# Attention and feed-forward on one core: the value products of a pair's fourth block and half block in one burst

## The chip, the core and the metric

One core of one Trainium2 chip runs the whole program. The metric is device time in microseconds (us), from the start of the program to its end. The engines are TensorE (PE: matrix products and transposes), VectorE (DVE), ScalarE (ACT), GpSimd (POOL) and SyncE (SP, which issues most of the transfers); each works through its own queue in order and waits for the others by semaphores.

## What is computed

Four batches of eight heads go through attention (queries are averaged two by two, so 576 rows of queries meet 1152 keys, with a head width of 64), and the result, 576 x 512 a batch, through a mixing step (the real part of a two-dimensional Fourier transform, added to its input), a normalisation and a feed-forward network of width 2048:

```python
def _attn_ref(q, k, v):
    q_pool = q.reshape(B, H, S // factor, factor, D).mean(axis=3)
    scores = scale * np.matmul(q_pool, k.transpose(0, 1, 3, 2))
    scores = scores - np.max(scores, axis=-1, keepdims=True)
    attn = np.exp(scores)
    attn = attn / (np.sum(attn, axis=-1, keepdims=True) + 1e-09)
    return np.matmul(attn, v)

def _moe_ref(x, w_ch1, w_ch2):
    mixed = np.real(np.fft.fft(np.fft.fft(x, axis=1), axis=2))
    u = x + mixed
    un = (u - np.mean(u)) / np.sqrt(np.var(u) + 1e-06)     # per row
    return u + np.maximum(un @ w_ch1, 0.0) @ w_ch2
```

All of it is float32; the weights come as 64 bit numbers and are converted on the chip.

## The kernel before

**Pairs and blocks.** The 32 heads are worked in 16 pairs (0 to 15). The 576 queries of a head are four blocks of 128 and a half block of 64. For block j = 0 to 3 each of the two heads has a tile of its own; for j = 4 the two half blocks share one tile. A tile goes through these steps:

- scores: three pieces of 384 keys, two products each (four for the half block's tile), L220, into slots of the PSUM pool `ps_t` (five slots); DVE copies each piece to the tile `sp` and takes the row's extreme (L222);
- exp of the whole 1152 columns on ACT (L234, `s_exp`), when all three pieces are there;
- transposes of 128 x 128 on PE (L247, `t_step`), four to a PSUM slot, each group copied to a tile `pt` (L250) by ACT, for the second head's second group by DVE. A block of two tiles has the groups 4, 4, 4, 4 and 2, the half block 4, 4 and 1. `pt` has six buffers;
- value products (L263, `av`): nine chunks of keys for each of the two heads, the first head into partitions 0 to 63 of the accumulator `po`, the second into 64 to 127. The moving side is 128 columns wide for a block and 64 for the half block. The only buffer of `ps_o` holds `po`; ACT copies it to `x` (L271).

The page calls the PSUM tiles by pool: `s` or `t` (pool `ps_t`), `f` (pool `ps_f`), `o` (the accumulator). PE's transposes of the first four pairs mostly go to `f`, later ones to `t`.

**The order.** It is written out by the generator `attention()`, one block after another: two score pieces of the next block, then `finish` (the value products of the block before), then the transposes of this block in groups, with two further score pieces of the next block after the first and after the second group, and at the end the exps of the next block (`exps()`). So the exp of a block stands on ACT behind the copies of the transposes of the block before, and on PE the transposes of a block have two score pieces of the next block and the value products of the block before ahead of them. In block 3 the next one is the half block, in the half block it is block 0 of the next pair.

**The planner.** Between the yields of `attention()` runs a planner. It keeps a clock `now` (nanoseconds, from the numbers that the generator yields, as 1950 for a block's value products and 1000 for the half block's), runs events whose time has come, as the softmax denominators' path (`den_recip`: a transpose D on PE at L280, two small transfers, and the multiplication of `x` by them), starts conversions of the weights (`convert`, from a clock of 60000 on, 32 in all, with ACT, DVE and POOL), and places work of finished batches: `mids` (Fourier step L505 and L513, normalisation L545 to L604) and `fills` (FFN blocks of 12 products, L699 to L701), the latter as far as `credit` goes, which grows with the yielded PE time. What is left of it stands behind the last pair.

**The conversions' buffers.** A conversion takes three tiles of 128 x 512 with the tag `cv` (four buffers) from the pool `cvp`. `todo` holds conversions that have not begun, `busy` those that run. In the trace, conversions run from pair 2 to pair 9.

Of the kernel before, what the change touches and what calls it, by code (L numbers as in the profile page):

```python
# [12 lines left out]
F32 = mybir.dt.float32  # L13
# [7 lines left out]
B, H, S, D = 4, 8, 1152, 64  # L21
# [3 lines left out]
P = 128  # L25
NKC = S // P
# [28 lines left out]
def fused_kernel(ctx: ExitStack, tc: tile.TileContext, k2, q2, v2, w1, w2, cst, out):  # L55
    nc = tc.nc
# [8 lines left out]
    ptp = pool("pt", 6)  # L65
    smp = pool("sm", 2)
    cvp = pool("cv", 1)
# [7 lines left out]
    ps_t = pool("ps_t", 5, space=PSUM)  # L75
    ps_o = pool("ps_o", 1, space=PSUM)
# [27 lines left out]
    qkv = {}  # L104
# [134 lines left out]
    def t_step(pr, items, eng):  # L239

        steps[0] += 1
        if pr < 4 and steps[0] % 5 != 2:
            ps = ps_f.tile([P, 512], F32, tag="f", name="f")
        else:
            ps = ps_t.tile([P, 512], F32, tag="t", name="t")
        for i, (k, c) in enumerate(items):
            nc.tensor.transpose(ps[:, i * P:i * P + P], sp[k][:, c * P:(c + 1) * P], ident)  # L247
        pt = ptp.tile([P, 512], F32, tag="pt", name="pt")
        o = len(items) * P
        (nc.vector.tensor_copy if eng == "v" else nc.scalar.copy)(pt[:, :o], ps[:, :o])  # L250
        return pt

    xt = {}
    started = []

    def av(pr, j, where):
        nonlocal now
        po = ps_o.tile([P, P], F32, tag="o", name="o")
        w = P if j < 4 else D
        for c in range(NKC):  # L260
            for y in range(2):
                pt, o = where[y, c]
                nc.tensor.matmul(po[y * D:y * D + D, :w], lhsT=qkv[2 * pr + y][3][:, c, :], rhs=pt[:, o:o + w],  # L263
                                 start=c == 0, stop=c == NKC - 1)
            if c in (2, 5) and j < 4:
                now += 650 * (c // 2)
                run_events()
                now -= 650 * (c // 2)
        if pr not in xt:
            xt[pr] = xt[pr + 1] = xp.tile([P, 2, SQ], F32, tag="x", name="x")  # L270
        nc.scalar.copy(xt[pr][:, pr % 2, j * P:j * P + w], po[:, :w])  # L271
# [40 lines left out]
    def attention():  # L312
# [35 lines left out]
        for i, (pr, j) in enumerate(units):  # L348
# [32 lines left out]
            def tr(items, eng):  # L381
                pt = t_step(pr, [(k, c) for k, c, _ in items], eng)
                for x, (_, _, ys) in enumerate(items):
                    for y, o in ys:
                        where[y, items[x][1]] = pt, x * P + o
                return 105 * len(items)
# [10 lines left out]
            if i:  # L397
                yield some(2)
                yield finish(*held)
# [12 lines left out]
            for k in tiles:  # L412
                sp.pop(k)
        yield finish(*held)

    def finish(pr, j, where):
        if j == 0 and pr % 2 == 0 and pr // 2 >= XB:

            drain(*divmod(pr // 2 - XB, 2))
        if j == 2 and pr % 2 and (pr + 1) // 2 >= XB and pr + 1 < NP:  # L420
            drain(*divmod((pr + 1) // 2 - XB, 2))
        av(pr, j, where)
        if j == 4:
            for y in range(2):
                qkv.pop(2 * pr + y)
        return 1950 if j < 4 else 1000


    ut = {}
# [234 lines left out]
    ORDER = [(w, q * GF + i) for q in range(NFC // GF) for w in range(2) for i in range(GF)]  # L664

    todo = deque(ORDER)
    busy = []
# [124 lines left out]
    now = due = credit = 0.0  # L792
# [11 lines left out]
    def run_events():  # L804
        while events and events[0][0] <= now:
            heapq.heappop(events)[2]()

    def drain(b, h):
        nonlocal now, due, credit
        while (b, 2 * h + 1) not in done_f2:  # L810
            if mids and now >= due:
                c = step(mids)
                if c:
                    now += c[0]
                    credit -= c[0]
                    due = now + c[1]
                continue
            c = step(fills)
            now += c or 300
            credit -= c  # L820
            conversions()
            run_events()
# [116 lines left out]
```

## Time and profile before

| | us |
|---|---|
| median of three runs | 1013.74 |
| the three runs | 1014.59, 1013.74, 1013.72 |
| the profiled execution | 1013.12 |
| its span, first to last instruction | 1011.4 |

| engine | busy us | share of the span |
|---|---|---|
| PE | 962.3 | 95% |
| DVE | 601.4 | 59% |
| ACT | 526.3 | 52% |
| POOL | 398.2 | 39% |

The pairs take the span up to 791 us, the rest of the feed-forward network the remaining 220. All times below are from the profiled execution and counted from its first instruction; what lies around the span (1.7 us) is no engine's work.

### The profile page before, as it was taken

The numbers are of one execution on the slowest core, as the hardware profiler recorded it, in microseconds if no ns is written. First come the engines' busy times: TensorE is split into PE (matmuls) and PEld (weight loads), VectorE is DVE, ScalarE is ACT, GpSimd is POOL, SyncE is SP. The second block draws the span as 40 slices with busy tenths as digits, with TensorE's granted clock in tenths as the row PEclk, the third lists the DMA queues.
The fourth block names the chain that finished last, engine by engine and source line by source line (L and its number), as shares of the span: only waits on it lengthen the run. The fifth ranks groups of instructions, "written<-read, shape, count | busy, mean of one in ns | idle before, by whom it ended". The sixth has DMA issues, their size and how long they took to land.

```text
span 1011.4 us, 19728 instructions
## 1 busy us (share of the span) xinstructions
PE 962.3 (95%) x7392; PEld 838.3 (83%) x7392; DVE 601.4 (59%) x1526; ACT 526.3 (52%) x1033; POOL 398.2 (39%) x577
## 2 busy tenths in 40 slices
PE   6999989798999998998999999999999999999998
PEld 5898888677788887776988888787988888899998
DVE  5557869789875597866544465745644275422222
ACT  5778868658865665655744454535844221301100
POOL 3555875868776667774523222222400000000000
PEclk9999999999999999999999999999999999999999
DMA  5645467556477775585765464354442445734432
GB/s 178 181 128 182 148 203 250 162 172 187 132 227 270 260 239 178 171 302 159 232 193 178 123 198 100 91 172 142 131 124 83 152 147 151 244 131 125 125 125 63
DMA packets 62515, 170.91 MB, mean 169 GB/s; under 512 B 16770, under 2 KB 20242, under 8 KB 62420
## 3 DMA queue, kind: packets, MB, share of 16 engines
q1 hardware_dynamic: 55924, 151.18, 47.5%
q0 software_dynamic: 4320, 17.70, 5.5%
q8 instruction: 58, 0.95, 0.4%
q10 hardware_dynamic: 2176, 0.79, 0.3%
q14 instruction: 37, 0.30, 0.1%
HBM read 146.88 MB, written 22.75 MB: 168 GB/s over the span
## 4 chain that ended last, share of the span: by engine, by line
PE 53%; DVE 2%; ACT 1%; issue 1%; POOL 0%; DVEq 0%; ACTq 0%
PE f L699 7%; PE f L701 6%; PE f L700 6%; PE s L220 6%; PE o L263 6%; PE t L247 5%; PE t L699 5%; PE t L701 5%; PE t L700 5%; DVE sp L222 1%; PE f L513 1%; PE t L513 1%; PE f L505 0%; ACT pt L250 0%; ACT sp L234 0%
## 5 line engine op out<-in xcount | busy, mean ns | idle before, releaser
L222 DVE TENSOR_SCALAR_CACHE_REDUCE sp<-s,bia 128x384 f32<-128x384 f32 x288 | 177.4, 616 | 88.0 <-PE s L220 65.2
L220 PE MATMUL s<-ks,qh 128*128 128x384 f32 x480 | 185.3, 386 | 16.9 <-ACT qh L164 6.1
L234 ACT ACTIVATE sp<-sp,bia 128x1152 f32<-128x1152 f32 x144 | 180.1, 1255 | 6.1 <-DVE sp L222 5.9
L250 ACT COPY pt<-t 128x512 f32<-128x512 f32 (+2 forms) x243 | 125.0, 527 | 109.6 <-PE t L247 108.3
L220 PE MATMUL s<-ks,ql 128*128 128x384 f32 x480 | 164.8, 343 | 2.6 <-POOL ql L197 2.6
L263 PE MATMUL o<-pt,vs 128*64 128x128 f32 (+1 forms) x2880 | 163.6, 267 | 1.4 <-DVE pt L250 1.2
L263 PEld LDWEIGHTS o<-pt,vs 128*64 128x64 f32 x2880 | 145.1, 138 | 23.4 <-issue 20.4
L247 PE MATMUL t<-ident,sp 128*128 128x128 f32 x1045 | 151.5, 277 | 7.2 <-ACT pt L250 3.5
L247 PEld LDWEIGHTS t<-ident,sp 128*128 128x128 f32 x1045 | 121.6, 141 | 28.0 <-issue 6.3
L189 POOL TENSOR_TENSOR ks<-kr,ks 64x288 fp32r<-64x288 f32 x120 | 99.3, 859 | 52.2 <-DMA ks<-in_k 21.6
L220 PEld LDWEIGHTS s<-ks,qh 128*128 128x128 f32 x480 | 92.6, 193 | 26.5 <-ACT qh L164 6.6
L220 PEld LDWEIGHTS s<-ks,ql 128*128 128x128 f32 x480 | 93.1, 194 | 3.8 <-POOL ql L197 2.8
L718 ACT ACTIVATE g<-f 128x512 fp32r<-128x512 f32 (+1 forms) x49 | 28.3, 577 | 120.1 <-PE f L701 120.1
L719 DVE SCALAR_TENSOR_TENSOR g<-f,g 128x512 fp32r<-128x512 f32 (+1 forms) x49 | 32.5, 663 | 97.0 <-ACT g L718 97.0
L197 POOL TENSOR_TENSOR ql<-qr,qh 128x288 fp32r<-128x288 f32 (+2 forms) x75 | 55.9, 770 | 77.2 <-ACT qh L194 76.2
L222 DVE TENSOR_SCALAR_CACHE_REDUCE sp<-s 128x384 f32<-128x384 f32 x144 | 78.6, 546 | 11.4 <-PE s L220 10.5
L653 POOL TENSOR_TENSOR rest<-rest,wa 128x256 f32<-128x256 f32 x64 | 50.0, 799 | 70.9 <-DVE wa L646 51.9
L699 PE MATMUL f<-g,w 128*128 128x512 f32 (+1 forms) x192 | 75.9, 396 | 2.0 <-PE f L585 1.0
L699 PE MATMUL f<-unh,w 128*128 128x512 f32 (+1 forms) x196 | 76.7, 391 | 0.9 <-DVE g L719 0.9
L701 PE MATMUL f<-unl,w 128*128 128x512 f32 (+1 forms) x196 | 74.6, 380 | 0.0
L700 PE MATMUL f<-unh,w 128*128 128x512 f32 (+1 forms) x196 | 74.2, 379 | 0.0
L701 PE MATMUL f<-g,w 128*128 128x512 f32 (+1 forms) x192 | 74.0, 385 | 0.0
(146 smaller groups left out, 1723.4 us busy)
## 6 DMA issues: line engine op xcount, KB each, us to landing
w<-w SPq DMA_DIRECT2D x128, 512.0 KB, 4.2
qr<-in_q SPq DMA_DIRECT2D x30, 576.0 KB, 5.8
ks<-in_k POOLq DMA_DIRECT2D x30, 576.0 KB, 6.5
wraw<-in_w SPq DMA_DIRECT2D x32, 512.0 KB, 4.1
w<-wraw SPq DMA_DIRECT2D x32, 512.0 KB, 2.6
vs<-in_v SPq DMA_DIRECT2D x32, 288.0 KB, 6.9
kr<-in_k SPq DMA_DIRECT2D x30, 288.0 KB, 7.2
out<-x SPq DMA_DIRECT2D x12, 256.0 KB, 2.0
```

The lines of the kernel that those rows point to most:

```text
L189: nc.gpsimd.tensor_tensor(ks[D:, c], kr[D:, c], ks[D:, c].bitcast(F32), op=ALU.subtract)
L197: nc.gpsimd.tensor_tensor(ql[:, z], qr[:, 0, x:y], qh[:, z].bitcast(F32), op=ALU.subtract)
L220: nc.tensor.matmul(ps, lhsT=l, rhs=k, start=i == 0, stop=i == len(ops) - 1)
L222: nc.vector.tensor_scalar(sp[n, j][:, c], ps, -0.0625, bt[:, pc - 1:pc] if pc else None, op0=ALU.mult, op1=ALU.min, accum_out=bt[:, pc:pc ...
L234: last_exp[0] = nc.scalar.activation(t, t, AF.Exp, bias=bia.pop((n, j))[:, 2:3], scale=-1.0, accum_out=den[pr][:, col:col + 1]).ins
L247: nc.tensor.transpose(ps[:, i * P:i * P + P], sp[k][:, c * P:(c + 1) * P], ident)
L250: (nc.vector.tensor_copy if eng == "v" else nc.scalar.copy)(pt[:, :o], ps[:, :o])
L263: nc.tensor.matmul(po[y * D:y * D + D, :w], lhsT=qkv[2 * pr + y][3][:, c, :], rhs=pt[:, o:o + w], start=c == 0, stop=c == NKC - 1)
L653: nc.gpsimd.tensor_tensor(o[:, c], x[:, c], y[:, c], op=op)
L699: nc.tensor.matmul(ps, lhsT=ah, rhs=bh, start=first, stop=False)
L700: nc.tensor.matmul(ps, lhsT=al, rhs=bh, start=False, stop=False)
L701: nc.tensor.matmul(ps, lhsT=ah, rhs=bl, start=False, stop=last)
```

## The change

In some pairs the value products of block 3 are not issued at their place. `finish` for j = 3 notes the block's `pt` tiles in `joined` and returns 0; when the half block's turn comes (j = 4), the new function `av_two` issues both: for each of the nine chunks, two products of block 3 into `po`, then two of the half block into a second accumulator `pb`, a slot of the pool `ps_t`. Two ACT copies to `x` follow. Pairs are joined if no conversion has begun and the planner's clock is below 60000, or if all conversions are through (`not todo and not busy`). The half block's three `pt` tiles of a joined pair come from the conversions' buffers (tag `cv`), because block 3's five stay in use. The planner counts 0 + 2700 for the two bursts in place of 1950 + 1000.

```diff
--- before.py
+++ after.py
@@ -245,13 +245,28 @@
             ps = ps_t.tile([P, 512], F32, tag="t", name="t")
         for i, (k, c) in enumerate(items):
             nc.tensor.transpose(ps[:, i * P:i * P + P], sp[k][:, c * P:(c + 1) * P], ident)
-        pt = ptp.tile([P, 512], F32, tag="pt", name="pt")
+        src = (cvp, "cv", 4) if pr in joined and items[0][0][1] == 4 else (ptp, "pt", 6)
+        pt = src[0].tile([P, 512], F32, tag=src[1], name="pt", bufs=src[2])
         o = len(items) * P
         (nc.vector.tensor_copy if eng == "v" else nc.scalar.copy)(pt[:, :o], ps[:, :o])
         return pt
 
     xt = {}
     started = []
+
+    joined = {}
+
+    def av_two(pr, where):
+        po = ps_o.tile([P, P], F32, tag="o", name="o")
+        pb = ps_t.tile([P, 512], F32, tag="t", name="t")
+        for c in range(NKC):
+            for p, w, at in ((po, P, joined[pr]), (pb, D, where)):
+                for y in range(2):
+                    pt, o = at[y, c]
+                    nc.tensor.matmul(p[y * D:y * D + D, :w], lhsT=qkv[2 * pr + y][3][:, c, :], rhs=pt[:, o:o + w],
+                                     start=c == 0, stop=c == NKC - 1)
+        nc.scalar.copy(xt[pr][:, pr % 2, 3 * P:4 * P], po[:, :P])
+        nc.scalar.copy(xt[pr][:, pr % 2, 4 * P:], pb[:, :D])
 
     def av(pr, j, where):
         nonlocal now
@@ -419,11 +434,17 @@
             drain(*divmod(pr // 2 - XB, 2))
         if j == 2 and pr % 2 and (pr + 1) // 2 >= XB and pr + 1 < NP:
             drain(*divmod((pr + 1) // 2 - XB, 2))
-        av(pr, j, where)
+        if j == 3 and (len(todo) == len(ORDER) and now < 60000 or not todo and not busy):
+            joined[pr] = where
+            return 0
+        if pr in joined:
+            av_two(pr, where)
+        else:
+            av(pr, j, where)
         if j == 4:
             for y in range(2):
                 qkv.pop(2 * pr + y)
-        return 1950 if j < 4 else 1000
+        return 1950 if j < 4 else 2700 if pr in joined else 1000
 
 
     ut = {}
```

The built program has nine joined pairs: 0, 1 and 9 to 15. On PE, in block 3 and the half block of pair 0 (the first that is joined), there stood before the last transposes of block 3, four score products (two pieces for the next pair), the value products of block 3 and the half block's first four transposes:

```order
L247 MATMUL f<-ident,sp 128x128 x10
L220 MATMUL s<-ks,qh 128x384
L220 MATMUL s<-ks,ql 128x384
L220 MATMUL s<-ks,qh 128x384
L220 MATMUL s<-ks,ql 128x384
L263 MATMUL o<-pt,vs 64x128 x18
L247 MATMUL f<-ident,sp 128x128 x4
```

Now the half block's transposes come straight behind the score products:

```order
L247 MATMUL f<-ident,sp 128x128 x10
L220 MATMUL s<-ks,qh 128x384
L220 MATMUL s<-ks,ql 128x384
L220 MATMUL s<-ks,qh 128x384
L220 MATMUL s<-ks,ql 128x384
L247 MATMUL f<-ident,sp 128x128 x4
```

And at the half block's turn, where 18 products of 64 x 64 stood, two score products are followed by two wide and two narrow products, nine times over:

```order
L220 MATMUL s<-ks,qh 128x384
L220 MATMUL s<-ks,ql 128x384
L266 MATMUL o<-pt,vs 64x128 x2
L266 MATMUL t<-pt,vs 64x64 x2
L266 MATMUL o<-pt,vs 64x128 x2
L266 MATMUL t<-pt,vs 64x64 x2
```

The 18 wide products have moved behind all of the half block's transposes; the same holds for the other eight joined pairs, in pairs 10 to 12 with FFN blocks elsewhere than before.

On ACT, pair 13 (block 2's copy to `x`, copies of block 3's transposes, casts `unh` of batch 2's normalisation, a load of the exp table, the half block's exp) was:

```order
L271 COPY x<-o 128x128
L250 COPY pt<-t 128x512
L603 CAST unh<-d 128x2x288
L250 COPY pt<-t 128x512 x2
L603 CAST unh<-d 128x2x288
L250 COPY pt<-t 128x256
L234 ACT_TABLE_LOAD
L234 ACTIVATE sp,den<-sp,bia 128x1152
```

and is now (lines behind the change have higher numbers, L603 is L624 and the copy to `pt` is L251):

```order
L286 COPY x<-o 128x128
L251 COPY pt<-t 128x512 x3
L624 CAST unh<-d 128x2x288
L251 COPY pt<-t 128x256
L624 CAST unh<-d 128x2x288
L234 ACT_TABLE_LOAD
L234 ACTIVATE sp,den<-sp,bia 128x1152
```

The two casts have moved behind three and four copies, the second right ahead of the table's load and the exp. In the other joined pairs the exp of the half block still follows the last copy of block 3's transposes.

On PE in pair 15, the last, which has no next pair, the transposes of block 3 (14), its value products and an FFN block stood before the half block's transposes:

```order
L247 MATMUL t<-ident,sp 128x128 x14
L263 MATMUL o<-pt,vs 64x128 x18
L699 MATMUL f<-g,w_9383 128x512
L700 MATMUL f<-g,w_9383 128x512
L701 MATMUL f<-g,w_9383 128x512
```

Now two transposes of block 3 and nine of the half block follow each other, then the joined burst; the FFN block stands ahead of them:

```order
L721 MATMUL f<-g,w_9338 128x512
L722 MATMUL f<-g,w_9338 128x512
L247 MATMUL t<-ident,sp 128x128 x11
L266 MATMUL o<-pt,vs 64x128 x2
L266 MATMUL t<-pt,vs 64x64 x2
L266 MATMUL o<-pt,vs 64x128 x2
```

The value products of block 3 no longer stand between the two blocks' transposes.

## Rows read from the trace of the kernel before

**Rows 1.** The page: busy us, share of the span and instructions of each engine.
```profile
PE 962.3 (95%) x7392; PEld 838.3 (83%) x7392; DVE 601.4 (59%) x1526; ACT 526.3 (52%) x1033; POOL 398.2 (39%) x577
```

**Rows 2.** Stretches in us: length, busy time by engine, PE's granted clock, DMA share, GB/s.
```profile
22.00:82.00 60.00, 59.07 (x634) 53.58 (x634) 35.98 (x118) 45.72 (x91) 33.88 (x54) 1.00 0.55 163
...
472.00:791.00 319.00, 315.18 (x2585) 272.00 (x2585) 169.12 (x463) 169.81 (x331) 80.31 (x125) 1.00 0.48 147
```

**Rows 3.** PE in order of time, pair 1: start us, us, line, operation, tiles, count.
```profile
71.98 0.43 PE L220 MATMUL s<-ks,qh 128*128 128x384 f32 x1
...
72.86 2.19 PE L263 MATMUL o<-pt,vs 128*64 128x128 f32 x36
74.98 0.66 PE L247 MATMUL f<-ident,sp 128*128 128x128 f32 x4
75.39 0.42 PE L220 MATMUL s<-ks,qh 128*128 128x384 f32 x1
...
76.18 0.60 PE L247 MATMUL f<-ident,sp 128*128 128x128 f32 x4
...
78.22 1.27 PE L263 MATMUL o<-pt,vs 128*64 128x64 f32 x36
79.42 0.66 PE L247 MATMUL t<-ident,sp 128*128 128x128 f32 x4
```

**Rows 4.** ACT in order of time, pair 1.
```profile
72.53 1.26 ACT L234 ACTIVATE sp<-sp,bia 128x1152 f32<-128x1152 f32 x1
...
79.04 1.24 ACT L234 ACTIVATE sp<-sp,bia 128x1152 f32<-128x1152 f32 x1
```

**Rows 5.** PE in order of time, pair 9; in brackets idle time and what ended it.
```profile
473.43 2.19 PE L263 MATMUL o<-pt,vs 128*64 128x128 f32 x36
475.91 0.66 PE L247 MATMUL t<-ident,sp 128*128 128x128 f32 x4 [0.30 <-ACT sp L234]
```

**Rows 6.** ACT in order of time, pair 9.
```profile
474.51 1.25 ACT L234 ACTIVATE sp<-sp,bia 128x1152 f32<-128x1152 f32 x1
```

**Rows 7.** PE in order of time, pair 13.
```profile
700.50 1.31 PE L263 MATMUL o<-pt,vs 128*64 128x128 f32 x18
...
703.23 0.66 PE L247 MATMUL t<-ident,sp 128*128 128x128 f32 x4
```

**Rows 8.** ACT in order of time, pair 13.
```profile
699.29 0.68 ACT L603 CAST unh<-d 128x576 fp32r<-128x576 f32 x1
...
700.26 1.28 ACT L234 ACT_TABLE_LOAD   x1
701.56 1.26 ACT L234 ACTIVATE sp<-sp,bia 128x1152 f32<-128x1152 f32 x1
```

**Rows 9.** PE in order of time, pair 15.
```profile
783.62 2.38 PE L263 MATMUL o<-pt,vs 128*64 128x128 f32 x36
785.92 0.50 PE L699 MATMUL f<-g,w 128*128 128x512 f32 x1
...
788.78 1.15 PE L247 MATMUL t<-ident,sp 128*128 128x128 f32 x9
790.11 1.29 PE L263 MATMUL o<-pt,vs 128*64 128x64 f32 x36 [0.18 <-ACT pt L250]
791.33 0.50 PE L699 MATMUL t<-g,w 128*128 128x512 f32 x1
```

**Rows 10.** ACT in order of time, pair 15.
```profile
783.99 1.26 ACT L234 ACTIVATE sp<-sp,bia 128x1152 f32<-128x1152 f32 x1
```

**Rows 11.** PE in order of time, pair 3, and a stretch there (columns as in rows 2).
```profile
138.05 0.66 PE L247 MATMUL f<-ident,sp 128*128 128x128 f32 x4 [2.62 <-ACT pt L250]
...
140.29 3.68 PE L263 MATMUL o<-pt,vs 128*64 128x128 f32 x36
143.90 0.66 PE L247 MATMUL f<-ident,sp 128*128 128x128 f32 x4
...
140.00:143.40 3.40, 3.40 (x32) 3.11 (x32) 2.16 (x6) 1.77 (x3) 1.76 (x3) 0.50 0.20 51
```

## The prediction

> **What bounds the kernel now.** I read the page first: TensorE (PE) is busy 95% of the span [rows 1]. The table by stretches shows where the rest is: from 82 to 472 us, where weights are converted, PE has its waits, but in the two stretches that the change touches it has none to speak of: 59.07 of 60 us busy over pairs 0 and 1, and 315.18 of 319 us from pair 9's fourth block to pair 15 [rows 2]. There the time is PE's instructions one after another, in the order in which they are written, so whatever PE waits for in addition is paid in full unless it replaces another wait. Then I followed one joined pair in order of time on PE [rows 3] and on ScalarE (ACT) [rows 4], looked for the joined pairs that differ from it (pair 9 [rows 5, 6], pair 13 [rows 7, 8], pair 15 [rows 9, 10]), and last at what a long gap does to PE's clock [rows 11].
>
> What the reader is to see in rows 3 and 4 is what the burst of the fourth block does for others. The transposes of the half block (T4, L247 at 74.98) need its exp. That exp starts on ACT at 72.53, after the copy of the fourth block's last transposes, and ends at 73.79 [rows 4]. PE has finished the two score pieces in between long before: they start at 71.98, and such a pair of pieces with transposes behind it takes 0.79 (75.39 to 76.18) [rows 3]. The value burst V of the fourth block, 72.86 to 74.98, is what PE does meanwhile. T4 never waits because V stands ahead of it.
>
> **What the order says.** Nine of 16 pairs are joined: 0 and 1, before the conversions, and 9 to 15, after them. In each, V leaves its place between the score pieces and T4, and its 18 products come back one block later, alternating with the half block's 18 (L266). Pairs 2 to 8 have the same order on all engines as before; after pair 9 some FFN blocks stand elsewhere.
>
> **The price of the joined burst.** No row shows 128 and 64 wide products alternating, so it is bounded. V takes 2.12 (72.86 to 74.98), the half burst v 1.20 (78.22 to 79.42) [rows 3]. They have the same number of loads and products (36 records, 18 for either half of the array) and differ only in columns, so half the columns are worth 0.92, and a burst is 0.28 fixed and 1.84 or 0.92 for columns. If none of the fixed part is saved the joined burst takes 3.32, if it is paid once 3.04, if it is hidden wholly 2.76. On the other side, if each narrow product takes as long as a wide one, 4.24. I take 3.17, halfway between once and twice: a part of 0.28 must be entering and leaving the burst, which is saved (the pieces before V take 0.88 from 71.98, and 0.79 ahead of transposes, so entering alone shows), and a part goes with every product, which isn't. [...]
>
> **A common pair** (0, 1, 10, 11, 12, 14). Without V, T4 comes when the exp is done: 72.53 + 1.26 = 73.79, and 0.14 to 0.15 for the signal (pair 9: exp from 474.51 for 1.25, T4 at 475.91 with ACT named as what it waited for [rows 5, 6]), so 73.93 in place of 74.98: 1.05 earlier. PE then stood still from 72.77 to 73.93, 1.16 that nothing covers: in pairs 0 and 1 there are no FFN blocks, and in pairs 10 to 12 the order has them ahead of the last two transposes or after T4, never between the score pieces and T4; ahead of the last transposes they delay the exp by as much. The transposes, score pieces and half block's copies behind T4 move with it. The burst then takes 3.17 in place of 1.20: 1.97 later. Sum 1.97 - 1.05 = +0.92, six times: +5.5. The burst of 3.17 covers the next pair's two exps better than v did, but they end at 79.04 + 1.24, and T4 at 79.42 needs only the first of them [rows 3, 4]: nothing was waited for there, so nothing comes back.
>
> **Pair 9.** ACT loads its exp table ahead of this exp, and T4 waits for the exp already (475.91 [rows 5]), V or no V. V's 2.12 ahead of it come free of charge now and must be paid later: 0 + 1.97 = +2.0.
>
> **Pair 13.** Here batch 2's normalisation runs. Today V starts at 700.50, T4 at 703.23; the exp (701.56 + 1.26, with the 1.28 table load at 700.26 ahead of it) allows it at 702.96 [rows 7, 8]. That gives 1.97 - 0.27 = +1.7. In the new order one more cast L603 (0.68) stands ahead of the exp, +2.4; but this stretch also has waits for VectorE (DVE) that a longer pause of PE lets it catch up with, down to the common +0.9. I take +1.5.
>
> **Pair 15.** There is no next pair's score, so the half block's nine transposes come straight behind the fourth block's. The exp runs 783.99 to 785.25 [rows 10], so they start 785.39 - 783.62 = 1.77 later than PE is ready. Then transposes 1.33 and burst 3.17: 6.27, against V 2.30, transposes 1.33 and v 1.22 today, 4.85 [rows 9]; the FFN block between them only changes place. +1.4.
>
> **What costs nothing.** The second copy to x (L269) stands on ACT behind the exps while PE goes on with transposes. The half accumulator takes a slot of the score pool; DVE has the time of the burst to empty the others. The half block's copies in the conversions' buffers: three of four, free again before pair 2's first conversion. The planner's clock runs 250 ns a pair less, so one FFN block (2.86 of PE, 785.92 to 788.78 [rows 9]) moves from between the pairs to the end: the same time in another place. The denominators' transpose D comes right behind the burst, its small DMA a little earlier against the rest. On GpSimd two multiplications of x move by one head's work; it is busy 80 of 319 us there [rows 2]. Of the 1.8 us by which pairs 2 to 8 start later, between none and all could be swallowed by their waits; I take none swallowed, since these waits are between engines whose queues are all delayed alike.
>
> **Sum.** 5.5 + 2.0 + 1.5 + 1.4 = 10.4 us. The profiled execution took 1013.12 us with a span of 1011.4, 0.6 below the median 1013.74 of the three runs; on the median: **1024 us**, about 1% slower.
>
> **Rivals.**
> - Swallowed waits. If the idle time PE has today in the joined pairs lies where a pause would replace it, at most 3.8 us go over pairs 9 to 15 and 0.9 over pairs 0 and 1 [rows 2], 4.7 in all: 1019.3. Against it: the common pair has no wait at all between V and T4 behind v.
> [...]
> - Narrow products as dear as wide ones: burst 4.24, 9 x 1.07 = +9.6, 1033.6. Against it: v itself is far shorter than V.
> - Faster. If a joined pair were paced by ACT or DVE, PE's 1.16 would replace idle time of PE, V's moving would be free, and only the saved fixed part would count: 9 x -0.28 = -2.5, 1011.2. It decides where PE idles over 1.16 us in a pair; rows 2 show some 0.5 on average. Only an exp that is ready earlier, or FFN work that lands in the gap, could bring this about, and the order shows neither.
> - The change does less than it says (fewer pairs joined, or the order undone at run time): excluded by the order, since each engine runs its queue as it stands; 9 bursts stand there.
>
> **How the numbers follow.** Forecast with its bounds for the burst (3.04 to 3.32, -1.2 to +1.4 in all) and for pair 13 (0.9 to 2.4): 1022 to 1026.5, 0.55. Swallowed waits or half-clock stretches that fall away, 1017 to 1022: 0.17. New half-clock stretches, 1026 to 1030: 0.13. Dear narrow products: 0.05. Within 0.2% (about 2 us, roughly what a measurement can tell from no change): 0.04. Faster: 0.06. The range 1018.5 to 1029.5 leaves some 0.18 outside. Faster by over 0.2% 0.06, same 0.04, slower 0.90.
>
> **What would show it.** Right: in the changed trace PE waits before the half block's first transposes, ACT's exp (L234) named, 1.1 to 1.2 us in pairs 0, 1, 10, 11, 12 and 14, some 2.5 in pairs 9 and 13, 1.8 in pair 15, about 14 us in all, where the trace before has 0.3; joined bursts of 3.0 to 3.3 us; the tail unchanged but for a block more. Wrong: bursts far from 3.17, no wait at those transposes, or granted clock at 0.50 in stretches behind them.

## The result and the profile after

The changed kernel takes 1024.23 us (median of five runs, 1022.00 to 1029.89); the kernel before 1013.74, of five runs too. The ratio is 1.0096, 95% interval 1.0073 to 1.0119: slower by about 1%, as forecast (1024.0). The profiled execution took 1024.23 us with a span of 1022.5, so 11.1 more than that of before; PE's mean granted clock was 0.993 of full speed (0.994 before).

PE's work is the same and its busy time a little less; the 11.1 us are standing still. The page, busy time and share of the span, against [rows 1]:

```profile
PE 960.6 (94%) x7392; PEld 838.2 (82%) x7392; DVE 598.8 (59%) x1526; ACT 527.0 (52%) x1033; POOL 396.8 (39%) x577
```

What PE waited for, by its line and the line that released it (us in total, times, longest). First after:

```profile
PE t L247 <- ACT sp L234: 12.0, 9, 3.0
...
PE f L247 <- ACT sp L234: 3.0, 3, 1.0
```

Then the same two of before:

```profile
PE f L247 <- ACT sp L234: 1.0, 1, 1.0
PE t L247 <- ACT sp L234: 0.9, 3, 0.4
```

Transposes waiting for an exp (L247 <- L234, in both pools' slots) went from 1.9 us to 15.0, by 13.1: more than the whole loss, and part of it in the place of other waits. Of the 15.0, 13.4 stand ahead of the half block's first transposes (T4) in the nine joined pairs, where before only pair 9 had one, of 0.3.

**A common pair.** Pair 1 after, PE in order of time (start, us, line, operation, tiles, count; in brackets idle time and what ended it), against [rows 3]:

```profile
73.01 0.42 PE L220 MATMUL s<-ks,qh 128*128 128x384 f32 x1
...
74.96 0.66 PE L247 MATMUL f<-ident,sp 128*128 128x128 f32 x4 [1.01 <-ACT sp L234]
...
78.21 0.44 PE L266 MATMUL o<-pt,vs 128*64 128x128 f32 x4
...
81.37 0.28 PE L295 MATMUL t<-ident,den 128*9 128x128 f32 x1
```

and ACT there, against [rows 4]:

```profile
73.56 1.26 ACT L234 ACTIVATE sp<-sp,bia 128x1152 f32<-128x1152 f32 x1
```

The exp ends at 74.82, T4 starts at 74.96. From the score pieces to T4 it is 1.95 us where two pieces take 0.79: a wait of 1.16. (The bracket counts idle time from the pieces' modelled end, hence 1.01.) The joined burst runs from 78.21 to 81.37, 3.16. The same 1.95 stands in pairs 0, 10, 12 and 14. In pair 11 it is 2.22: there an FFN activation (L739, at 568.28) stands on ACT ahead of the copy and the exp.

**Pair 9.** PE, then ACT, against [rows 5, 6]: the exp table's load stands ahead of the exp, and PE stands still for 3.36 - 0.79 = 2.57 us.

```profile
474.68 0.43 PE L220 MATMUL s<-ks,qh 128*128 128x384 f32 x1
...
478.04 0.66 PE L247 MATMUL t<-ident,sp 128*128 128x128 f32 x4 [2.42 <-ACT sp L234]
```

```profile
475.35 1.28 ACT L234 ACT_TABLE_LOAD   x1
476.64 1.25 ACT L234 ACTIVATE sp<-sp,bia 128x1152 f32<-128x1152 f32 x1
```

**Pair 13.** PE, against [rows 7]. Two products of the normalisation (L606) end the queue ahead of the wait:

```profile
705.91 0.65 PE L606 MATMUL f<-dg,onesm 96*128 96x288 f32 x2
709.51 1.11 PE L247 MATMUL t<-ident,sp 128*128 128x128 f32 x4 [2.95 <-ACT sp L234]
710.28 0.67 PE L220 MATMUL s<-ks,qh 128*128 128x384 f32 x1
...
711.71 0.91 PE L247 MATMUL t<-ident,sp 128*128 128x128 f32 x4
712.37 0.42 PE L220 MATMUL s<-ks,qh 128*128 128x384 f32 x1
```

ACT, against [rows 8]: the cast (now L624) stands ahead of the table's load, as the order said.

```profile
706.11 0.69 ACT L624 CAST unh<-d 128x576 fp32r<-128x576 f32 x1
706.82 1.28 ACT L234 ACT_TABLE_LOAD   x1
708.11 1.25 ACT L234 ACTIVATE sp<-sp,bia 128x1152 f32<-128x1152 f32 x1
```

And the stretches in which PE's clock was granted at half (columns as in [rows 2]; the granted clock is the 0.50 ahead of the DMA share). There are three, at 138.90, 183.27 and 708.92. The last lies here, and begins while PE still waits:

```profile
138.90:145.73 6.83, 5.83 (x38) 5.06 (x40) 3.27 (x8) 4.66 (x11) 4.73 (x7) 0.50 0.53 174
...
708.92:712.33 3.41, 2.82 (x11) 2.73 (x12) 2.06 (x6) 1.12 (x3) 2.20 (x3) 0.50 0.02 5
```

In it a group of four transposes and the two pieces behind it took 2.20 us (709.51 to 711.71); in pair 1 the same takes 1.20. Before, the stretches were three too (a fourth takes the last 1.0 us of the span, where PE no longer works), but the third was not in a joined half block (at 460.83).

**Pair 15.** PE, against [rows 9]. Two transposes of block 3, then 1.7 us for the exp, nine of the half block, the burst (3.16):

```profile
792.87 0.38 PE L247 MATMUL t<-ident,sp 128*128 128x128 f32 x2
794.96 1.20 PE L247 MATMUL t<-ident,sp 128*128 128x128 f32 x9 [1.71 <-ACT sp L234]
796.09 0.44 PE L266 MATMUL o<-pt,vs 128*64 128x128 f32 x4
...
799.25 0.28 PE L295 MATMUL t<-ident,den 128*9 128x128 f32 x1
```

**Pair 10**, a common pair by the forecast, lost less. In the kernel before, the half block's last pieces there had waits that pair 1 lacks (a piece has 0.17 to the next, a single transpose 0.03):

```profile
516.33 0.34 PE L220 MATMUL s<-ks,ql 128*128 128x384 f32 x1
516.70 0.33 PE L247 MATMUL t<-ident,sp 128*128 128x128 f32 x1
...
517.06 0.33 PE L220 MATMUL s<-ks,ql 128*128 128x384 f32 x1
517.38 0.44 PE L220 MATMUL s<-ks,qh 128*128 128x384 f32 x1
```

After, the same place runs without them. The rows of DVE speak for the FFN block as the reason, not for PE's pause. Before, DVE multiplies for an FFN block (L719) ahead of its copies of the pieces, and after, that block stands behind the single transpose (516.75) and the copies begin at 515.44. First before, then after:

```profile
515.50 0.69 DVE L719 SCALAR_TENSOR_TENSOR g<-f,g 128x512 fp32r<-128x512 f32 x1 [4.68 <-ACT g L718]
516.11 0.61 DVE L222 TENSOR_SCALAR_CACHE_REDUCE sp<-s,bia 128x384 f32<-128x384 f32 x1
```

```profile
515.44 0.62 DVE L222 TENSOR_SCALAR_CACHE_REDUCE sp<-s,bia 128x384 f32<-128x384 f32 x1 [1.02 <-PE s L220]
```

**Pair 12** lost more, and there it is the other way round: now an FFN block's multiplication stands ahead of DVE's copies, and the single transpose and the piece behind it wait 0.27 and 0.45 us for them (DVE's rows first, then PE's):

```profile
627.89 0.69 DVE L740 SCALAR_TENSOR_TENSOR g<-f,g 128x512 fp32r<-128x512 f32 x1 [2.63 <-ACT g L739]
628.50 0.61 DVE L222 TENSOR_SCALAR_CACHE_REDUCE sp<-s,bia 128x384 f32<-128x384 f32 x1
```

```profile
628.73 0.34 PE L220 MATMUL s<-ks,ql 128*128 128x384 f32 x1
629.17 0.33 PE L247 MATMUL t<-ident,sp 128*128 128x128 f32 x1
629.65 0.44 PE L220 MATMUL s<-ks,qh 128*128 128x384 f32 x1
```

No run moves FFN blocks alone, so for both pairs this is read from rows and not tested. (For the wait at 516.70 the profile names ACT's copy of the group before, which ends at 516.65; after, the transpose starts at 516.73 with that copy running to 516.81, so it isn't that.)

Worked out over PE's rows from the score pieces behind block 3's transposes (in pair 15, from the transposes' end) to the end of the last value burst, with the FFN blocks and the Fourier step left out, and pair 13's L606 products taken off at the 0.59 that such a pair of products takes ahead of transposes elsewhere (701.95 to 702.54):

| pair | before us | after us | more | forecast |
|---|---|---|---|---|
| 0, 1 (each) | 7.44 | 8.36 | 0.92 | 0.92 |
| 9 | 7.82 | 9.78 | 1.96 | 2.0 |
| 10 | 7.97 | 8.25 | 0.28 | 0.92 |
| 11 | 7.68 | 8.61 | 0.9 | 0.92 |
| 12 | 7.35 | 8.99 | 1.6 | 0.92 |
| 13 | 8.77 | 11.64 | 2.9 | 1.5 |
| 14 | 7.53 | 8.36 | 0.83 | 0.92 |
| 15 | 4.85 | 6.25 | 1.4 | 1.4 |

Together 11.7. Pairs 2 to 8, worked in the order of before, add 0.46, the program's start 0.15; what is left, the other blocks of pairs 9 to 15 and the tail, then comes out 1.2 shorter, a remainder that no single row shows. The tail has one FFN block more, which stood between pairs before.

### The profile page after: what moved, and what is told of

The parts are those of the page before. It is cut to its first block, busy times and chain, and to the rows that moved or that the text cites. A ratio compares the mean times of both kernels' runs of the same rounds, so it can differ in the third digit from the quotient of the medians.

```text
span 1022.5 us, 19714 instructions
## 1 busy us (share of the span) xinstructions
PE 960.6 (94%) x7392; PEld 838.2 (82%) x7392; DVE 598.8 (59%) x1526; ACT 527.0 (52%) x1033; POOL 396.8 (39%) x577
## 4 chain that ended last, share of the span: by engine, by line
PE 53%; ACT 2%; issue 1%; DVE 1%; POOL 0%; DVEq 0%; ACTq 0%
PE f L720 6%; PE f L722 6%; PE f L721 6%; PE s L220 6%; PE t L247 5%; PE t L720 5%; PE t L721 5%; PE t L722 5%; PE o L278 4%; PE o L266 1%; PE f L534 1%; ACT sp L234 1%; PE t L266 1%; ACT pt L251 1%; DVE sp L222 0%
## 5 line engine op out<-in xcount | busy, mean ns | idle before, releaser
L251 ACT COPY pt<-t 128x512 f32<-128x512 f32 (+2 forms) x243 | 125.1, 527 | 119.4 <-PE t L247 118.3
L234 ACT ACTIVATE sp<-sp,bia 128x1152 f32<-128x1152 f32 x144 | 180.0, 1254 | 5.5 <-DVE sp L222 5.3
L247 PE MATMUL t<-ident,sp 128*128 128x128 f32 x1045 | 152.6, 278 | 18.1 <-ACT sp L234 12.0
L247 PEld LDWEIGHTS t<-ident,sp 128*128 128x128 f32 x1045 | 122.7, 142 | 39.9 <-ACT sp L234 14.9
L278 PE MATMUL o<-pt,vs 128*64 128x128 f32 (+1 forms) x2232 | 132.0, 272 | 0.7 <-DVE pt L251 0.7
L278 PEld LDWEIGHTS o<-pt,vs 128*64 128x64 f32 x2232 | 117.1, 138 | 17.7 <-issue 16.2
L739 ACT ACTIVATE g<-f 128x512 fp32r<-128x512 f32 (+1 forms) x48 | 27.6, 575 | 121.5 <-PE f L722 121.5
L720 PE MATMUL f<-g,w 128*128 128x512 f32 (+1 forms) x192 | 75.7, 394 | 3.2 <-issue 2.1
L720 PE MATMUL f<-unh,w 128*128 128x512 f32 (+1 forms) x192 | 75.1, 391 | 0.9 <-DVE g L740 0.9
L722 PE MATMUL f<-g,w 128*128 128x512 f32 (+1 forms) x192 | 73.4, 382 | 0.0
L721 PE MATMUL f<-g,w 128*128 128x512 f32 (+1 forms) x192 | 73.0, 380 | 0.0
```

The costliest lines, as they stand in the source:

```text
L234: last_exp[0] = nc.scalar.activation(t, t, AF.Exp, bias=bia.pop((n, j))[:, 2:3], scale=-1.0, accum_out=den[pr][:, col:col + 1]).ins
L720: nc.tensor.matmul(ps, lhsT=ah, rhs=bh, start=first, stop=False)
L721: nc.tensor.matmul(ps, lhsT=al, rhs=bh, start=False, stop=False)
L722: nc.tensor.matmul(ps, lhsT=ah, rhs=bl, start=False, stop=last)
```

## Experiments

Each experiment is compared with the kernel before on the same chip: 1014.45 (e1 to e4) and 1014.52 us (e5 to e8), from some 25 runs each. The time given is the median, the ratio is to the kernel before, with its 95% interval. Diffs are against the changed kernel where nothing else is said.

**e1: the buffers alone.** The kernel before, with only the half block's tiles of the nine pairs moved to the conversions' buffers.

```diff
-        pt = ptp.tile([P, 512], F32, tag="pt", name="pt")
+        src = (cvp, "cv", 4) if items[0][0][1] == 4 and (pr < 2 or pr > 8) else (ptp, "pt", 6)
+        pt = src[0].tile([P, 512], F32, tag=src[1], name="pt", bufs=src[2])
```

> The kernel before with one part of the change alone: the half block's tiles of pairs 0, 1 and 9 to 15 lie in the conversions' buffers; nothing is joined and PE's order is that of before. If the loss is PE's wait for the half block's exp, the buffers cost nothing: 1013.7 us, within 2. If the buffers (a wait for a slot that a conversion held) were the cause, up to 1024.

1014.86 us, ratio 0.9998 (0.9986 to 1.0009), and PE's waits for an exp are those of before:

```profile
PE f L247 <- ACT sp L234: 1.0, 1, 1.0
...
PE t L247 <- ACT sp L234: 1.0, 3, 0.5
```

The buffers cost nothing that shows (0.1% at most); the loss is in the joining.

**e2: only pairs 0 and 1 joined.**

```diff
-        if j == 3 and (len(todo) == len(ORDER) and now < 60000 or not todo and not busy):
+        if j == 3 and len(todo) == len(ORDER) and now < 60000:
```

> The changed kernel with pairs 0 and 1 joined alone. Theory of the wait: two waits of 1.16 us and two bursts of 3.16, 0.9 a pair, all of it kept through pairs 2 to 8: 1015.5 us. If the conversions' waits swallow the delay: 1013.7. If the planner's shifted clock and the FFN blocks that move after pair 9 were the cause, also 1013.7, and no wait to be seen.

1015.19 us, ratio 1.001 (0.9992 to 1.0027). In the trace both pairs have the 1.95 ahead of T4 and bursts of 3.16, 0.92 lost in each. Pair 1 nevertheless ends only 0.92 later than before (80.34 against 79.42 in [rows 3]), because this execution was 0.87 ahead before the first joined burst, at its first transposes (13.28 against 14.15). Pair 8 ends 0.49 later, at 405.39 against 404.90. So in this one profile 0.43 was given back where the conversions run. The interval is too wide to tell a loss of 1.8 us from none; in the changed kernel itself pairs 2 to 8 gave nothing back but lost 0.46 more.

**e3: the two bursts behind one another, not alternating.**

```diff
-        for c in range(NKC):
-            for p, w, at in ((po, P, joined[pr]), (pb, D, where)):
+        for p, w, at in ((po, P, joined[pr]), (pb, D, where)):
+            for c in range(NKC):
```

> The changed kernel with the joined burst in another order: all 18 wide products, then all 18 narrow ones. If what is saved is entering and leaving one burst less, it takes 3.16 us as before and the time stays at 1024. If alternating hides the narrow products' loads under the wide ones, it takes 3.25 to 3.32 here, in all 1 to 1.5 us more.

1026.06 us, ratio 1.0108 (1.0072 to 1.0143), not to be told from the changed kernel. Pair 1 on PE:

```profile
77.97 2.19 PE L266 MATMUL o<-pt,vs 128*64 128x128 f32 x36
79.98 1.22 PE L266 MATMUL t<-pt,vs 128*64 128x64 f32 x36
81.13 0.28 PE L295 MATMUL t<-ident,den 128*9 128x128 f32 x1
```

2.01 + 1.15 = 3.16, the same as alternating, in all nine pairs. So the 0.16 saved against 2.12 + 1.20 comes of nothing standing between the two; the alternation adds nothing to it.

**e4: a short exp.** In the nine pairs the half block's exp works 128 of its 1152 columns.

```diff
+        if j == 4 and (pr < 2 or pr > 8):
+            t = t[:, :128]
```

> The changed kernel with the half block's exp in the nine joined pairs cut to its first 128 of 1152 columns (the rest of that tile goes on without exp, so part of the computation is left out); order of all engines unchanged. Theory of the wait: the exp takes some 0.35 us in place of 1.26, the wait ahead of the half block's transposes falls from 1.16 to some 0.25, nine times 0.9 less: 1016 us. If the joined burst, the buffers or the moved FFN blocks were the cause, it stays at 1024.

1016.88 us, ratio 1.0021 (1.0002 to 1.004): of the 1% that the changed kernel loses, some fifth is left, with the order of the changed kernel and bursts of 3.16 as there. (The other 1024 columns go on without exp.) Pair 1 on PE, and the exp on ACT (lines stand two lower in this kernel):

```profile
71.16 0.42 PE L220 MATMUL s<-ks,qh 128*128 128x384 f32 x1
...
72.26 0.66 PE L249 MATMUL f<-ident,sp 128*128 128x128 f32 x4 [0.16 <-ACT sp L236]
```

```profile
71.71 0.41 ACT L236 ACTIVATE sp<-sp,bia 128x128 f32<-128x128 f32 x1
```

The exp is 0.85 shorter and T4 comes 0.85 sooner (1.10 behind the pieces' start in place of 1.95). The table's load stays in pairs 9 and 13, and so do waits there (1.6 and 2.1).

**e5: four score pieces ahead of T4 in place of two.**

```diff
+                if j == 4 and pr in joined:
+                    yield some(2)
```

> The changed kernel with four score pieces in place of two ahead of the half block's first transposes in joined pairs (the other two come where the two after the first group stood). Theory of the wait: four pieces take 1.57 us in place of 0.79, the wait of 1.16 falls to 0.4, in eight of nine pairs (pair 15 has no pieces): 6 us less, 1018. If VectorE or the score pool's five slots become the bound, the pieces or the second group wait instead and little is won: 1022 or more.

1018.89 us, ratio 1.004 (1.0022 to 1.0058). Pair 1 on PE: 1.96 us from the first of the four to T4, where four take 1.57, so a wait of about 0.4 in place of 1.16.

```profile
71.94 0.42 PE L220 MATMUL s<-ks,qh 128*128 128x384 f32 x1
...
73.90 0.66 PE L247 MATMUL f<-ident,sp 128*128 128x128 f32 x4 [0.31 <-ACT sp L234]
```

Score pieces cover what V covered, as far as they reach. In pair 9 it was still 3.36, with the table's load.

**e6: the exp one copy earlier**, ahead of the copy of block 3's last two transposes.

```diff
+                if j == 3 and y == 0 and (pr < 2 or pr > 8):
+                    exps()
```

> The changed kernel with the half block's exp of joined pairs put on ACT one copy earlier, ahead of the copy of the last two transposes (and beside the copy that VectorE makes). Theory of the wait: it starts some 0.6 us earlier, the wait falls from 1.16 to 0.5 in the common pairs, by as much in pairs 9 and 13, and goes in pair 15, where an FFN block now lies behind the exp: 6 to 7 us less, 1017.5. If the wait has another cause than the exp's end, or the late copy makes a PSUM slot late instead: 1022 to 1024.

1018.09 us, ratio 1.0042 (1.0024 to 1.006). In pair 1 T4 comes 1.54 behind the pieces' start, a wait of 0.75:

```profile
71.02 0.42 PE L220 MATMUL s<-ks,qh 128*128 128x384 f32 x1
...
72.56 0.66 PE L247 MATMUL f<-ident,sp 128*128 128x128 f32 x4 [0.59 <-ACT sp L234]
```

**e7: both, e5 and e6.**

> The changed kernel with both: exp ahead of the last copy and four score pieces ahead of the half block's transposes. Theory of the wait: none is left in the common pairs and pair 15, some 1.3 us in pairs 9 and 13, where ACT loads its table first; what is left of the change is one burst entered and left less, 0.25 us a pair: 1014, the kernel before within 2. If something else than the wait was the cause: over 1018.

1017.45 us, ratio 1.0034 (1.0018 to 1.005), 3 us above what was expected. In the common pairs the wait is gone: in pair 1 four pieces and T4 follow without a break, and the half block takes 7.24 us (72.35 to 79.59) against 7.44 before.

```profile
72.35 0.42 PE L220 MATMUL s<-ks,qh 128*128 128x384 f32 x1
...
73.89 0.66 PE L247 MATMUL f<-ident,sp 128*128 128x128 f32 x4
...
79.59 0.28 PE L295 MATMUL t<-ident,den 128*9 128x128 f32 x1
```

What is left stands mostly in pairs 9 and 13. In pair 9 the wait is 1.4 (2.98 for four pieces). In pair 13 there are now several waits, for queries that were not ready, a copy and DVE, and half clock behind them, from 708.01 for 3.41 us (columns as above):

```profile
702.90 0.41 PE L220 MATMUL s<-ks,qh 128*128 128x384 f32 x1 [0.80 <-POOL qr L186]
...
704.12 0.66 PE L247 MATMUL t<-ident,sp 128*128 128x128 f32 x4 [0.63 <-ACT pt L251]
...
705.45 0.44 PE L220 MATMUL s<-ks,qh 128*128 128x384 f32 x1 [0.67 <-ACT pt L251]
```

```profile
708.01:711.42 3.41, 3.34 (x21) 2.62 (x23) 3.25 (x13) 2.97 (x6) 0.00 (x0) 0.50 0.00 0
```

**e8: e7 without pairs 9 and 13**, an attempt at a version faster than both.

```diff
-                if j == 3 and y == 0 and (pr < 2 or pr > 8):
+                if j == 3 and y == 0 and (pr < 2 or pr > 9 and pr != 13):
...
-        if j == 3 and (len(todo) == len(ORDER) and now < 60000 or not todo and not busy):
+        if j == 3 and pr not in (9, 13) and (len(todo) == len(ORDER) and now < 60000 or not todo and not busy):
```

> As the one with both, but pairs 9 and 13, where ACT loads its table ahead of the half block's exp, are not joined. Theory of the wait: no new wait is left, seven bursts fewer of 0.25 us: 1012, 0.2% below the kernel before at best; with VectorE or PSUM slots as the new bound in some pairs: 1014.

1015.21 us, ratio 1.0005 (0.9988 to 1.0022): not to be told from the kernel before, and no gain. Its median is 2.2 below e7's, so the two pairs with a table's load cost about that much even with both covers (in e7's pair 13 with a half-clock stretch). The 0.2 us that a covered pair saves makes 1.4 over seven pairs, an estimate from pair 1 of e7; the interval neither shows nor excludes it. In e8's profile a wait for the exp is back in pair 15, 1.32 ahead of its half block (786.99): the FFN block that follows this exp in e7 stands elsewhere. That alone is as much as the seven pairs would save.

## Why the prediction was right, and where it was off

The sign and the mechanism held, and the time lies where it was forecast; that it came within 0.2 us (1024.0 against 1024.23) is luck, as the five runs lie 8 us apart and the terms erred both ways. By its own steps:

- **The joined burst**: 3.17 forecast between 3.04 and 3.32, 3.16 measured. Some 0.16 of the 0.28 is saved, as taken. The prediction took the middle of two bounds; e3 shows what it is, one burst entered and left in place of two. The bound of 3.04, with the fixed part paid once, does not come out, and no gain from narrow loads hidden under wide products shows: alternating and separate bursts both take 3.16. In the trace before a load took 137 ns (median) for these 64 columns and 140 for the 128 of a transpose.
- **The common pair**: the wait of 1.16 for the exp stands in pairs 0, 1, 10, 12 and 14, and the sum of +0.92 held within 0.1 in pairs 0, 1, 11 and 14. In pair 11 this is by compensation: a wait 0.27 longer, and 0.24 more before than in pair 1. Pair 10 was 0.28 and pair 12 1.6. The prediction put FFN blocks that change place at nothing ("the same time in another place"); by DVE's rows above, a block that now stands behind those pieces took some 0.4 us of waits out of pair 10, and one that now stands ahead of them brought 0.7 into pair 12. Another 0.2 in pair 10 is the denominators' transpose, which stood ahead of v and now stands behind the burst. Pair 12's Fourier step moved out of the half block too, so its two rows are not quite the same work.
- **Pair 9**: +1.96 for +2.0. V was free there before, since the exp behind its table load (1.28 from 473.22 in the trace before) made T4 wait anyway (0.30, [rows 5]), and had to be paid later.
- **Pair 13**: 2.9 for 1.5. Some 1.3 of it is the half-clock stretch at 708.92 (T4, two pieces and T4's next group took 0.77, 1.43 and 0.67 for 0.41, 0.79 and 0.35), for which the prediction had a chance of 0.13 and nothing in the sum. Without it 1.6 is left, the term as forecast.
- **Pair 15**: +1.4 for +1.4.
- **What costs nothing**: the buffers, by e1; the FFN block that moved to the tail.
- **Pairs 2 to 8**: none swallowed, as taken, and 0.46 added; e2's profile shows that this can fall otherwise.

So the sum of 10.4 came out at 11.1 by compensation too: pair 10's -0.6 and the remainder of -1.2 against pairs 12 and 13 and the 0.46 of pairs 2 to 8. That the waits for the exp are the cause, and not the order of the products or the buffers, is shown by e4 (shorter exp, same order: 0.2% left of 1%) and by e5 to e7 (other work or an earlier exp in V's place: 0.3 to 0.4% left). The prediction said that the trace before had 0.3 us of such waits: right for the half block's transposes, in pair 9; the 1.9 above have three waits of other blocks besides.

The chance given to new half-clock stretches (1026 to 1030) came true in one place. Of the two long new waits, 2.6 in pair 9 had no half clock behind it (the granted clock was 1.00 from 478 to 486), and 3.0 in pair 13 had it in this execution. The other profiles do not tie it to the length of the wait. From the normalisation's two products to T4, pair 13 took 3.60 here and 3.61 in e3, where no half clock followed; it took 2.75 in e6, with half clock from 704.16 on, and 2.76 in e4, without. So pair 13's wait was followed by half clock in two of five profiles (after and e6, not e3, e4 and e5), and no run shows that a wait brings it, nor what a new stretch costs in general: in the one of [rows 11] a V took 3.61 (143.90 - 140.29) in place of 2.12, 1.5 more, and the one of pair 13 cost 1.3. Nor did a stretch that falls away give back 1.5: the one at 460.83 is gone (after, the granted clock was 1.00 from 460.90 to 464.20), and the second of two FFN blocks there starts 5.14 us behind the first (467.00 - 461.86) where it was 5.15 (464.85 - 459.70).

## What to carry to other kernels

A burst that nobody waits for can still be doing a job: covering another engine's latency for the instruction queued behind it. Before moving one, find the next instruction's own input and when it is ready; the wait that the burst hid (here 1.16 us against the 0.16 saved) becomes visible, unless other ready work is put in its place, as the four score pieces were (a wait of about 0.4 in place of 1.16, e5). Where such a gap is long already, as in pairs 9 and 13 with a table's load, leave the burst where it is (e8 against e7, 2.2 us). And work that only changes place can still change what stands ahead of another engine's copies, as the FFN blocks in pairs 10 and 12 (by the rows, some 0.4 us less and 0.7 more of waits).

## What was not expected of the hardware

The granted clock fell to 0.50 in stretches of 3.41 or 6.83 us at places that differ between profiles of nearly the same order. In e7 the one at 708.01 came behind waits of 0.55 to 0.80, where the changed kernel had one of 3.0. In e2's profile they stood at nearly the same three places as before (140.85, 181.81 and 461.71 against 139.98, 180.94 and 460.83), and so they did in e3's (141.13, 182.09 and 461.98), which has nine joined pairs as the changed kernel has; the order of the work does not settle where they fall. The single times of the changed kernel, 1022.00 to 1029.89, go with it in part: the two longest runs of the five had mean granted clocks of 0.987 and 0.988, the three others 0.992 to 0.995. Differences of 1 or 2 us in this kernel are therefore not read from one run.
